# Converting a tuned kernel's weights with two VectorE steps a piece: absolute value on ScalarE, a limit on GpSimd, shift and sign on VectorE

## The chip, the cores and the metric

The kernel runs on one core of a Trainium2 chip. The metric is the device time in microseconds (us) of one execution. All runs told of here were of the fast state or, where a kernel ran once, of unknown state; a profiled run says where its time went. Engines: PE is TensorE's matmul, PEld its weight load, DVE is VectorE, ACT ScalarE, POOL GpSimd, SPq SyncE's DMA queue.

## The reference

```python
def _attn_ref(q, k, v, tau):                 # (8, 8, 576, 64) each
    scores = scale * np.matmul(q, k.transpose(0, 1, 3, 2))
    thresh = np.max(scores, axis=-1, keepdims=True) - tau
    scores = np.where(scores >= thresh, scores, -1000000000.0)
    ...                                      # softmax, times v
def _moe_ref(x, w_tok1, w_tok2, w_ch1, w_ch2):   # x is (8, 576, 512)
    h = np.maximum(x.transpose(0, 2, 1) @ w_tok1, 0.0) @ w_tok2
    u = x + h.transpose(0, 2, 1)
    return u + np.maximum(u @ w_ch1, 0.0) @ w_ch2
```

The four weight matrices are float64: a float32 array times a double-precision scalar gives float64. The kernel makes float32 out of the two 32-bit words of each weight. That conversion is all that the change touches.

## The kernel before

The weights come in 31 pieces of at most 128x512. A piece is loaded into one of four raw buffers, ScalarE shortens the low word and squares the high word, VectorE builds the bits in three steps, and GpSimd adds the low part. The function `weight(n)` issues the next n VectorE steps with what belongs to them; the loop over 144 units of attention calls it at two or three places in each unit. (The code here and below is cut: guards for pieces that are not float64 and lines that only name buffers are left out.)

```python
    def on_scalar(i, part):
            if part == 0:
                nc.scalar.activation(out=lo.bitcast(I32), in_=lo, func=AF.Copy, scale=2.0**-29)
            else:
                nc.scalar.activation(out=h2, in_=hi.bitcast(F32), func=AF.Square)

    def on_vector(i, part):
            if part == 0:        # L201: shift out three exponent bits
                nc.vector.tensor_scalar(
                    out=bits, in0=hi, scalar1=3, scalar2=0x3FFFFFFF, op0=ALU.logical_shift_left, op1=ALU.bitwise_and)
            elif part == 1:      # L205: sign and top exponent bit
                nc.vector.scalar_tensor_tensor(
                    out=bits, in0=hi, scalar=0xC0000000, in1=bits, op0=ALU.bitwise_and, op1=ALU.bitwise_or)
            else:                # L209: tiny weights become zero
                nc.vector.scalar_tensor_tensor(out=dst, in0=h2, scalar=2.0**-30, in1=dst, op0=ALU.is_ge, op1=ALU.mult)

    def on_gpsimd(i):            # L215: add the low word's part
                nc.gpsimd.tensor_tensor(out=dst.bitcast(I32), in0=dst.bitcast(I32), in1=..., op=ALU.add)

    def weight(n):
        for k in range(steps_done, min(steps_done + n, 3 * len(pieces) + 1)):
            i, part = divmod(k, 3)
            if part == 0:
                on_gpsimd(i - 1)
                if i:
                    load_piece(i - 1 + NRAW)
            else:
                on_scalar(i + 1, part - 1)
            on_vector(i, part)
            steps_done = k + 1
```

A unit, cut to the order in which things are issued (each engine runs its own instructions in this order):

```python
    for u in range(len(units) + LAG + 4):
        scores(u)                 # PE scores, DVE row maximum (mx), POOL bias
        norm(u - 1)               # DVE reciprocal (rr), POOL scaling of e
        weight(2)                 # from the second batch on; before, by a schedule
        ...
        fill(0.4)                 # PE: channel and token work of the batch before
        turn_blocks(w)            # DVE transposition T, at every third unit 16 transfers eT<-T
        weight(2)
        weigh(u)                  # ACT: e = activations of the scores, frees their PSUM
        weight(2)
```

The scores lie in PSUM, the memory that TensorE writes to. Unit 24's scores need the tiles that unit 23's activations free; so a late ScalarE holds TensorE up.

Of the kernel before, what the change touches and what calls it, by code (L numbers as in the profile page):

```python
# [9 lines left out]
F32 = mybir.dt.float32  # L10
U32 = mybir.dt.uint32
I32 = mybir.dt.int32
I64 = mybir.dt.int64
AF = mybir.ActivationFunctionType
ALU = mybir.AluOpType
# [6 lines left out]
def kernel(  # L22
# [25 lines left out]
    nc = tc.nc  # L48
# [92 lines left out]
    def like(x, dst):  # L141
# [4 lines left out]
    pieces = [  # L146
        (w1[:, 2 * i : 2 * i + 2, :], moe_w_tok1[2 * P * i : 2 * P * i + 2 * P, :].rearrange("(t p) x -> p t x", p=P))
        for i in range(NI // 2)
    ]
# [12 lines left out]



    raws = {}

    def load_piece(i):
        if i >= len(pieces):
            return
        dst, src = pieces[i]  # L170
        rows = dst.shape[0]
        n = 1
        for d in dst.shape[1:]:
            n *= d
        raw = raw_at[i % NRAW][0:rows, 0 : n * (2 if wide(i) else 1)].bitcast(src.dtype)
        nc.sync.dma_start(out=like(raw, dst), in_=src)
        if wide(i):
            words = raw.bitcast(U32).rearrange("p (n w) -> p n w", w=2)
            h2 = work.tile([P, WMAX], F32, tag="o", name=f"h2_{i}")[0:rows, 0:n]
            raws[i] = like(words[:, :, 0], dst), like(words[:, :, 1], dst), like(h2, dst)  # L180
        else:
            raws[i] = like(raw, dst)

    def wide(i):
        return i < len(pieces) and pieces[i][1].dtype == I64

    def on_scalar(i, part):
        if wide(i):
            lo, hi, h2 = raws[i]
            if part == 0:  # L190
                nc.scalar.activation(out=lo.bitcast(I32), in_=lo, func=AF.Copy, scale=2.0**-29)
            else:
                nc.scalar.activation(out=h2, in_=hi.bitcast(F32), func=AF.Square)

    def on_vector(i, part):
        if wide(i):
            dst = pieces[i][0]
            lo, hi, h2 = raws[i]
            bits = dst.bitcast(U32)
            if part == 0:  # L200
                nc.vector.tensor_scalar(  # L201
                    out=bits, in0=hi, scalar1=3, scalar2=0x3FFFFFFF, op0=ALU.logical_shift_left, op1=ALU.bitwise_and
                )
            elif part == 1:
                nc.vector.scalar_tensor_tensor(  # L205
                    out=bits, in0=hi, scalar=0xC0000000, in1=bits, op0=ALU.bitwise_and, op1=ALU.bitwise_or
                )
            else:
                nc.vector.scalar_tensor_tensor(out=dst, in0=h2, scalar=2.0**-30, in1=dst, op0=ALU.is_ge, op1=ALU.mult)  # L209

    def on_gpsimd(i):
        if i >= 0:
            dst = pieces[i][0]
            if wide(i):
                nc.gpsimd.tensor_tensor(out=dst.bitcast(I32), in0=dst.bitcast(I32), in1=raws.pop(i)[0].bitcast(I32), op=ALU.add)  # L215
            else:
                nc.gpsimd.tensor_copy(out=dst, in_=raws.pop(i))
# [3 lines left out]
    steps_done = 0  # L221

    def weight(n):

        nonlocal steps_done
        for k in range(steps_done, min(steps_done + n, 3 * len(pieces) + 1)):
            i, part = divmod(k, 3)
            if part == 0:
                on_gpsimd(i - 1)
                if i:  # L230
                    load_piece(i - 1 + NRAW)
            else:
                on_scalar(i + 1, part - 1)
            on_vector(i, part)
            steps_done = k + 1

    def weight_to(x):

        weight(max(int(x) - steps_done, 0))

    def need(i):

        weight(3 * i + 4 - steps_done)

    load_piece(0)
    load_v(0)
# [29 lines left out]
    def in_blocks(b):  # L276
        return b > 0
# [10 lines left out]
    def scores(u):  # L288
        b, p0, t = units[u]
        sc = [  # L290
            (ps_3rd if b == 0 and (2 * u + h) % 3 == 2 else ps_sc).tile([P, 2, MAIN], F32, tag="sc", name=f"sc{h}_{u}") for h in range(2)
        ]
        if t == SHARED:
            parts = [(b * NP + p0, slice(MAIN, S), slice(0, 64)), (b * NP + p0 + 1, slice(0, LAST), slice(64, P))]
        else:
            o = P * t if t < SHARED else LAST + P * (t - SHARED - 1)
            parts = [(b * NP + p0 + (t > SHARED), slice(o, o + P), slice(0, P))]
        order = [(f, part, h) for f in range(2) for part in parts for h in range(2)]
        for f, (n, cols, rows), h in order if b else sorted(order, key=lambda o: o[2]):
            r = slice(D * h, D * h + D)  # L300
            qT, kT = heads[n]
            nc.tensor.matmul(sc[h][rows, f, 0:HS], lhsT=qT[r, cols], rhs=kT[r, HS * f : HS * f + HS], start=True, stop=True)  # L302
        mx = small.tile([P, 2], F32, tag="mx", name=f"mx_{u}")
        bias = small.tile([P, 2], F32, tag="bias", name=f"bias_{u}")
        for h in range(2):
            c = slice(h, h + 1)
            nc.vector.tensor_reduce(out=mx[:, c], in_=sc[h][:, :, 0:HS], axis=AX.XY, op=ALU.max)  # L307
            nc.gpsimd.tensor_scalar(out=bias[:, c], in0=mx[:, c], scalar1=toff, scalar2=-SCALE, op0=ALU.add, op1=ALU.mult)  # L308
        st[u] = sc, bias
# [66 lines left out]
    def split_middle(n):  # L376

        lv, vl = vals[n], vlast[n % VL]
        for h in range(2):
            r = slice(D * h, D * h + D)  # L380
            nc.gpsimd.tensor_copy(out=vl[r, r], in_=lv[r, NI, :])
        vals[n] = lv, vl
# [154 lines left out]
    def values_due(u):  # L537
        while due and due[0][0] <= u:
            _, b, p0, g = due.popleft()
            values(b, p0, g)  # L540
            if p0 == NP - 2 and g == 2:
                if not in_blocks(b):
                    return True
                push(b)
        return False

    for u in range(len(units) + LAG + 4):
        on = u < len(units)
        if u == UB:
            late.close()  # L550
            ps_mm = ctx.enter_context(tc.tile_pool(name="ps_mm", bufs=2, space=bass.MemoryType.PSUM))
        if on:
            b_now, p0, t = units[u]
            n = b_now * NP + p0
        w = u - LAG
        back = 0 <= w < len(units)
        if on:
            scores(u)

        last = False  # L560
        if due and not in_blocks(due[0][1]):
            last = values_due(u)
        if 0 < u <= len(units):
            norm(u - 1)
        if b_now:
            weight(2)
        else:

            weight_to(2.25 * (u - 1.5))
        while copies:  # L570
            copies.popleft()()
        if last:
            push(0)
        if back:
            wb, wp, wt = units[w]
            if not in_blocks(wb):
                for i in range(3):
                    turn(w, i)
            if wt % GU == GU - 1:
                g = wt // GU  # L580
                if g < 2:
                    split_middle(wb * NP + wp + g)
                due.append((u + (2 if in_blocks(wb) else 1), wb, wp, g))
        if b_now:
            fill(0.4)
        if back and in_blocks(wb):
            turn_blocks(w)
        if b_now:
            weight(2)
        if on:  # L590
            weigh(u)
        elif b_now:
            fill(0.6)
        if b_now:
            weight(2)
        elif u == 0:
            on_scalar(0, 0)
            on_scalar(0, 1)
        else:
            weight_to(2.25 * (u - 1))  # L600
        if on:


            when = {3: (2, 0, 2), 4: (2, 2, 4), 5: (2, 4, 6), 6: (2, 6, 8), 8: (3, 0, 3), 0: (1, 3, 6), 1: (1, 6, 8)}
            if u == 0:
                load_qk(1, (nc.sync, nc.sync), range(0, 3))
            if t in when:
                m, lo, hi = when[t]
                if n + m < len(pairs):
                    load_qk(n + m, (nc.scalar if b_now else nc.sync,) * 2, range(lo, hi))  # L610
            if t in (3, 7) and n + 2 + t // 4 < len(pairs):
                load_v(n + 2 + t // 4)
            if t == 2:
                prep(n + 1)
            if t == 7 and n + 2 < len(pairs):
                prep(n + 2)
        if due and in_blocks(due[0][1]):
            values_due(u)
# [31 lines left out]
```

## Time and profile before

| | before |
|---|---|
| time, median (lowest to highest) | 1379.77 us (1378.82 to 1380.43), 3 runs |
| TensorE busy, of the span of 1375.1 us | 96% |
| TensorE idle from 13.75 to 206 us | 35.7 us |
| TensorE idle from 206 us to the end | 9.4 us |

The prediction shows the lines. How to read them: in the busy tenths by slice, TensorE below 9 marks the stretch in which it often waits for other engines. In an instruction row come start, duration, engine, line, operation, output and input, and in square brackets the idle time before it and what ended it.

### The profile page before, as it was taken

To read this page: it belongs to the slowest core of one execution; us is meant where nothing else is said; L and a number is where in the kernel's file an instruction comes from. 1 tells how busy PE (TensorE), PEld (TensorE's weight loads), DVE (VectorE), ACT (ScalarE), POOL (GpSimd) and SP (SyncE) were. 2 spreads that over 40 slices of the span, in tenths; PEclk is the share of its full clock that TensorE was granted. 3 is DMA by queue.
4 is the path that set the end of the run, shared out by engine and by line. 5 is a ranking of instruction groups with operands and counts; after the bars stand their busy time and mean duration, and the time that the engine had idled before them with its cause. 6 is when DMAs were issued, how large, how long until landed. Compare 5 with 4: busy or idle time off the path is not lost.

```text
span 1375.1 us, 17691 instructions
## 1 busy us (share of the span) xinstructions
PE 1322.7 (96%) x6226; PEld 817.9 (59%) x6226; DVE 588.2 (43%) x1017; ACT 581.8 (42%) x1288; POOL 356.0 (26%) x683
## 2 busy tenths in 40 slices
PE   6877799999999999999999999999999999999998
PEld 3444465646565666565665567565656576575675
DVE  6788875445444443434244444434333453201000
ACT  5666654454445444443434444353333444120110
POOL 4555653222222222222122222222121222100000
PEclk9988999999999999999999999999999999999999
DMA  5434655454544354433344435434433442400000
GB/s 121 98 96 125 183 142 124 100 123 98 122 109 114 82 121 94 113 88 95 77 100 94 113 77 123 106 83 98 103 87 75 107 103 63 115 1 16 8 11 21
DMA packets 278871, 128.20 MB, mean 93 GB/s; under 512 B 200896, under 2 KB 271552, under 8 KB 278784
## 3 DMA queue, kind: packets, MB, share of 16 engines
q1 hardware_dynamic: 150176, 111.06, 32.0%
q10 hardware_dynamic: 128608, 16.01, 7.3%
q8 instruction: 50, 0.82, 0.3%
q14 instruction: 37, 0.30, 0.1%
HBM read 43.25 MB, written 9.44 MB: 38 GB/s over the span
## 4 chain that ended last, share of the span: by engine, by line
PE 85%; DVE 7%; DMA 2%; SPq 2%; ACT 1%; issue 1%; POOL 1%; ACTq 0%; DVEq 0%; POOLq 0%
PE c L486 26%; PE c L470 26%; PE sc L302 11%; PE pv L413 9%; PE t L441 5%; PE t L448 3%; PE pv L408 3%; DVE mx L307 2%; SPq L374 2%; PE tx L432 1%; PE c L482 1%; DMA eT<-T 1%; PE tr L353 1%; DVE wc L205 1%; ACT e L317 1%
## 5 line engine op out<-in xcount | busy, mean ns | idle before, releaser
L307 DVE TENSOR_REDUCE mx<-sc 128x1 f32<-128x576 f32 x288 | 204.5, 751 | 487.9 <-PE sc L302 487.5
L470 PE MATMUL c<-xT,wc 128*128 128x256 f32 (+1 forms) x1920 | 399.4, 362 | 2.1 <-DVE xT L452 1.2
L486 PE MATMUL c<-wc,g 128*128 128x512 f32 x864 | 390.5, 597 | 0.0
L470 PEld LDWEIGHTS c<-xT,wc 128*128 128x128 f32 x1920 | 334.5, 191 | 71.5 <-issue 27.6
L308 POOL TENSOR_SCALAR bias<-mx,toff 128x1 f32<-128x1 f32 x288 | 82.8, 288 | 799.3 <-DVE mx L307 742.3
L317 ACT ACTIVATE e<-sc,bias 128x576 f32<-128x576 f32 x288 | 199.6, 739 | 162.0 <-POOL bias L308 161.4
L486 PEld LDWEIGHTS c<-wc,g 128*128 128x128 f32 x864 | 157.8, 190 | 175.7 <-issue 174.0
L471 ACT ACTIVATE g<-c 128x256 f32<-128x256 f32 (+1 forms) x240 | 86.7, 362 | 334.1 <-PE c L470 317.9
L324 ACT ACTIVATE e<-e,ntau 128x576 f32<-128x576 f32 x288 | 220.7, 771 | 0.0
L335 POOL TENSOR_SCALAR e<-e,rr 128x576 f32<-128x576 f32 x288 | 215.6, 761 | 15.8 <-DVE rr L332 4.3
L302 PE MATMUL sc<-kT,qT 64*128 64x288 f32 (+1 forms) x1280 | 196.6, 447 | 11.1 <-DVE kT L284 7.1
L365 DVE STREAM_TRANSPOSE T<-e 128x1152 f32<-128x1152 f32 x126 | 172.1, 1366 | 6.3 <-DMA eT<-T 2.6
L302 PEld LDWEIGHTS sc<-kT,qT 64*128 64x128 f32 (+1 forms) x1280 | 107.4, 184 | 98.3 <-issue 59.1
L413 PE MATMUL pv<-eT,lv 128*64 128x384 f32 (+1 forms) x1024 | 136.8, 409 | 0.0
L413 PEld LDWEIGHTS pv<-eT,lv 128*64 128x64 f32 x1024 | 76.1, 138 | 51.0 <-issue 43.6
L491 DVE COPY o<-c 128x512 f32<-128x512 f32 x36 | 24.9, 692 | 177.5 <-PE c L486 177.5
L418 ACT COPY xT<-pv 128x384 f32<-128x384 f32 (+1 forms) x56 | 21.0, 401 | 157.5 <-PE pv L413 157.5
L448 PE MATMUL t<-w,a 128*128 128x288 f32 x256 | 75.2, 421 | 7.2 <-DVE xT L452 5.3
L441 PE MATMUL t<-x_sb,w 128*128 128x512 f32 x160 | 72.1, 598 | 0.0
L448 PEld LDWEIGHTS t<-w,a 128*128 128x128 f32 x256 | 45.6, 191 | 32.2 <-issue 11.4
L452 DVE TENSOR_TENSOR xT<-xT,t 128x288 f32<-128x288 f32 x64 | 28.2, 446 | 80.5 <-PE t L448 80.0
L324 ACT ACTIVATION_READ_ACCUMULATOR e<-e,ntau 128x1 f32 x288 | 56.5, 196 | 0.0
(44 smaller groups left out, 554.7 us busy)
## 6 DMA issues: line engine op xcount, KB each, us to landing
eT<-T SPq DMA_DIRECT2D x672, 108.0 KB, 2.2
scratch<-in_moe_w_ch_dram SPq DMA_DIRECT2D x24, 512.0 KB, 3.7
lv<-in_v_dram SPq DMA_DIRECT2D x32, 288.0 KB, 3.3
out_dram<-o SPq DMA_DIRECT2D x36, 256.0 KB, 2.2
lk<-in_k_dram ACTq DMA_DIRECT2D x111, 72.0 KB, 2.6
lq<-in_q_dram ACTq DMA_DIRECT2D x106, 72.0 KB, 2.3
lq<-in_q_dram SPq DMA_DIRECT2D x22, 72.0 KB, 3.2
lk<-in_k_dram SPq DMA_DIRECT2D x17, 72.0 KB, 3.3
```

Source lines behind the costliest of these rows:

```text
L302: nc.tensor.matmul(sc[h][rows, f, 0:HS], lhsT=qT[r, cols], rhs=kT[r, HS * f : HS * f + HS], start=True, stop=True)
L307: nc.vector.tensor_reduce(out=mx[:, c], in_=sc[h][:, :, 0:HS], axis=AX.XY, op=ALU.max)
L317: nc.scalar.activation(out=eh, in_=sc[h][:, :, 0:HS], func=AF.Prelu, bias=bias[:, h : h + 1], scale=SCALE, alpha=STEEP)
L324: nc.scalar.activation(out=eh, in_=eh, func=AF.Exp, bias=ntau, accum_out=rs[:, h : h + 1])
L335: nc.gpsimd.tensor_scalar(out=eh, in0=eh, scalar1=rr[:, h : h + 1], scalar2=1.0, op0=ALU.mult, op1=ALU.mult)
L365: nc.vector.transpose(out=T[:, :, place, :].rearrange("p a (c x) -> p c a x", c=NK), in_=e.rearrange("p (c a x) -> p c a x", c=NK, a=4))
L413: nc.tensor.matmul(to[r], lhsT=lv[:, j, :], rhs=e[j], start=False, stop=(c == NI - 1), skip_group_check=True)
L441: nc.tensor.matmul(ps, lhsT=w1[:, t, P * m : P * m + P], rhs=x_sb[:, t, :], start=(t == 0), stop=(t == NT - 1))
L448: nc.tensor.matmul(ps, lhsT=s["a"][:, m, P * c : P * c + P], rhs=w2[:, m, HS * f : HS * f + HS], start=(m == 0), stop=(m == NTK - 1))
L470: nc.tensor.matmul(ps, lhsT=wc1[:, j, c, :], rhs=uT[:, c, GR * i : GR * i + n], start=(c == 0), stop=(c == NCC - 1))
L471: nc.scalar.activation(out=s["g"][:, j, 0:n], in_=ps, func=AF.Relu)
L486: nc.tensor.matmul(flat, lhsT=s["g"][:, j, P * t : P * t + P], rhs=wc2[:, j, :], start=False, stop=(j == NJ - 1), skip_group_check=True)
```

## The change

The intent is to relieve VectorE: with |high word| times 2^16 instead of the square, and a limit from below at 2.0 instead of a mask, a plain shift gives all exponent bits, and one OR adds the sign. The third VectorE step goes; the limit goes to GpSimd.

```diff
             else:
-                nc.scalar.activation(out=h2, in_=hi.bitcast(F32), func=AF.Square)
+                nc.scalar.activation(out=h2, in_=hi.bitcast(F32), func=AF.Abs, scale=2.0**16)
...
             if part == 0:
-                    out=bits, in0=hi, scalar1=3, scalar2=0x3FFFFFFF, op0=ALU.logical_shift_left, op1=ALU.bitwise_and
+                    out=bits, in0=h2.bitcast(U32), scalar1=3, scalar2=0, op0=ALU.logical_shift_left, op1=ALU.bitwise_or
-            elif part == 1:
-                    out=bits, in0=hi, scalar=0xC0000000, in1=bits, op0=ALU.bitwise_and, op1=ALU.bitwise_or
             else:
-                nc.vector.scalar_tensor_tensor(out=dst, in0=h2, scalar=2.0**-30, in1=dst, op0=ALU.is_ge, op1=ALU.mult)
+                    out=bits, in0=hi, scalar=0x80000000, in1=bits, op0=ALU.bitwise_and, op1=ALU.bitwise_or
+
+    def on_gpsimd_first(i):
+            nc.gpsimd.tensor_scalar(out=h2, in0=h2, scalar1=2.0, scalar2=1.0, op0=ALU.max, op1=ALU.mult)
...
-            i, part = divmod(k, 3)
+            i, part = divmod(k, 2)
             if part == 0:
                 on_gpsimd(i - 1)
                 if i:
                     load_piece(i - 1 + NRAW)
-            else:
-                on_scalar(i + 1, part - 1)
+            on_scalar(i + 1, 1 - part)
             on_vector(i, part)
+            if part:
+                on_gpsimd_first(i + 1)
...
         if b_now:
-            weight(2)          # at the second and the third place of a unit
+            weight(1)
```

(The calls in the first batch change from 2.25 to 1.5 steps a unit. Pieces a unit stay the same everywhere.)

More of the change, by code (lines that the diff above doesn't have):

```diff
@@ L201, in on_vector @@
                 nc.vector.tensor_scalar(
-                    out=bits, in0=hi, scalar1=3, scalar2=0x3FFFFFFF, op0=ALU.logical_shift_left, op1=ALU.bitwise_and
-                )
-            elif part == 1:
-                nc.vector.scalar_tensor_tensor(
-                    out=bits, in0=hi, scalar=0xC0000000, in1=bits, op0=ALU.bitwise_and, op1=ALU.bitwise_or
-                )
-            else:
-                nc.vector.scalar_tensor_tensor(out=dst, in0=h2, scalar=2.0**-30, in1=dst, op0=ALU.is_ge, op1=ALU.mult)
+                    out=bits, in0=h2.bitcast(U32), scalar1=3, scalar2=0, op0=ALU.logical_shift_left, op1=ALU.bitwise_or
+                )
+            else:
+                nc.vector.scalar_tensor_tensor(
+                    out=bits, in0=hi, scalar=0x80000000, in1=bits, op0=ALU.bitwise_and, op1=ALU.bitwise_or
+                )
+    def on_gpsimd_first(i):
+        if wide(i):
+            h2 = raws[i][2]
+            nc.gpsimd.tensor_scalar(out=h2, in0=h2, scalar1=2.0, scalar2=1.0, op0=ALU.max, op1=ALU.mult)
     def on_gpsimd(i):
@@ L225, in weight @@
         nonlocal steps_done
-        for k in range(steps_done, min(steps_done + n, 3 * len(pieces) + 1)):
-            i, part = divmod(k, 3)
+        for k in range(steps_done, min(steps_done + n, 2 * len(pieces) + 1)):
+            i, part = divmod(k, 2)
             if part == 0:
@@ L241, in need @@
     def need(i):
-        weight(3 * i + 4 - steps_done)
+        weight(2 * i + 3 - steps_done)
     load_piece(0)
@@ L567 @@
         else:
-            weight_to(2.25 * (u - 1.5))
+            weight_to(1.5 * (u - 1.5))
         while copies:
@@ L594 @@
         if b_now:
-            weight(2)
+            weight(1)
         elif u == 0:
@@ L598 @@
             on_scalar(0, 1)
+            on_gpsimd_first(0)
         else:
-            weight_to(2.25 * (u - 1))
+            weight_to(1.5 * (u - 1))
         if on:
```

## The prediction

> **What bounds the kernel now.** I read the page's busy shares first, then its slices, then a table of busy time by stretch, then the groups and instructions of the stretch that the change touches.
>
> ```profile
> PE 1322.7 (96%) x6226; PEld 817.9 (59%) x6226; DVE 588.2 (43%) x1017; ACT 581.8 (42%) x1288; POOL 356.0 (26%) x683
> ...
> PE   6877799999999999999999999999999999999998
> ...
> DVE  6788875445444443434244444434333453201000
> ```
>
> TensorE is busy 96% of the span, so over most of it nothing that VectorE saves can count. Only the first six slices (34 us each, to 206 us) show TensorE at 6 to 8 tenths with VectorE at 7 to 8. There the weights are converted: 31 pieces, the last three-step piece at 198 us. After that TensorE is the bound, so a microsecond of TensorE idleness won or lost before 206 us should arrive at the end nearly whole.
>
> ```profile
> 13.75:106.18 92.43, 74.25 (x434) 44.42 (x432) 74.68 (x159) 62.53 (x131) 52.69 (x86) 0.91 0.38 86
> 106.18:206.00 99.82, 82.29 (x380) 50.76 (x379) 83.89 (x129) 62.99 (x131) 59.13 (x68) 0.91 0.59 154
> ```
>
> This is busy time of PE, PEld, DVE, ACT, POOL in two stretches, then the clock. From 13.75 to 106 us (the first pair of batches) TensorE is idle 18 us of 92, from 106 to 206 us 17.5 us of 100. So 35 us, 2.6% of the run, is all that a perfect conversion could win.
>
> In the second stretch VectorE and GpSimd stand in each other's way. One unit of attention there, VectorE in order of time, then GpSimd:
>
> ```profile
> 138.49 0.65 DVE L209 SCALAR_TENSOR_TENSOR wc<-h,wc 128x512 f32<-128x512 f32 x1
> 139.06 1.51 DVE L201 TENSOR_SCALAR wc<-scratch 128x512 uint32<-128x512 uint32 x1
> 140.60 1.66 DVE L205 SCALAR_TENSOR_TENSOR wc<-scratch,wc 128x512 uint32<-128x512 uint32 x1
> 142.37 0.69 DVE L209 SCALAR_TENSOR_TENSOR wc<-h,wc 128x512 f32<-128x512 f32 x1
> ```
> ```profile
> 138.49 3.22 POOL L215 TENSOR_TENSOR wc<-wc,scratch 128x512 int32<-128x512 int32 x2
> ```
>
> The shift takes 0.41 us alone and 1.51 here; the OR 0.70 alone and 1.66 here: each waits until one GpSimd addition is over.
>
> The third view is ScalarE and the SP DMA queue around the first block transposition:
>
> ```profile
> 148.63 12.19 SPq L374 DMA_DIRECT2D eT<-T  x16
> 160.93 19.33 SPq L176 DMA_DIRECT2D scratch<-in_moe_w_ch_dram  x6
> 180.48 10.38 SPq L374 DMA_DIRECT2D eT<-T  x16
> 190.97 0.52 SPq L176 DMA_DIRECT2D scratch<-in_moe_w_ch_dram  x1
> ```
> ```profile
> 154.55 0.74 ACT L317 ACTIVATE e<-sc,bias 128x576 f32<-128x576 f32 x1 [0.82 <-POOL bias L308]
> ...
> 165.20 0.69 ACT L191 ACTIVATE scratch<-scratch 128x512 int32<-128x512 uint32 x1 [2.82 <-DMA scratch<-in_moe_w_ch_dram]
> ```
>
> Sixteen transfers of T hold the queue 10 to 12 us; the weight load behind them (piece 24, issued 160.93) lands only at 165.2, and piece 30 (issued 190.97) at 194.6. ScalarE, in order, waits for each, but in the kernel before this comes **behind** its activations of unit 23 (154.55), so they are not held.
>
> **What the Trainium skill says.** "SBUF — State Buffer", section "Who interferes with whom": VectorE and GpSimd share a port pair as an exclusive lock; a VectorE instruction in a 2-port mode, or with two SBUF inputs against a GpSimd reader, blocks or is blocked for the whole instruction. The 1.51 and 1.66 us above agree. "VectorE: DVE Perf Modes", section "Mode 2×_2P": a one-source fp32 tensor_scalar in SBUF makes two results a cycle; the shift's 0.41 against the OR's 0.70 us fits. So both remaining VectorE steps can still be blocked. "ScalarE: Activation LUTs", section "Table sets: the hidden batching unit": abs lies in every table set; the trace has one table load, and the built instruction stream of the changed kernel has one too, so Abs for Square should cost nothing.
>
> **The change part by part.**
>
> Removed: the masking multiply L209, 31 times, 24 pieces at a mean of 0.83 us (20.0 us) and 7 smaller (4.0 us): 24 us of VectorE. Kept: shift and OR, at the old durations. Changed on ScalarE: Abs for Square, 0.66 us each, no difference. Added: a GpSimd tensor_scalar per piece. From L335, 128x576 in 0.73 us alone, I take 0.66 us for 512 columns and 0.4 for 288: about 19 us of GpSimd.
>
> First stretch (12 pieces, 1.5 steps a unit in place of 2.25). The chain that ended last, read from 10 to 106 us, holds 3.2 us of L201, 3.8 of L205 and 2.1 of L209, 9 us in all. One step in three goes: about 3 us won. Piece 0's limit now stands before unit 1's bias on GpSimd, about 0.7 us lost. Net -2.5 us.
>
> Second stretch (19 pieces, two a unit). Before, a unit from 114.74 to 123.29 us has VectorE full. After it: reduction 1.42, reciprocal 0.4, shift and OR 1.1, copies or transposition 1.4. Then the second shift waits for GpSimd: norm 1.97, addition 1.3, limit 0.7 put that at about 4.3 us after the reciprocals begin, where the second addition (1.3) takes the lock. Shift, OR and a collision with the next limit bring the next reduction at 8.4 to 8.9 us, against 8.55. So the saved VectorE step is **lost to the lock and to the wait for the limit**: 0, give or take 3 us over the stretch.
>
> Order on ScalarE. The instruction order of the built changed kernel shows the Abs of the second piece of a unit *ahead* of that unit's attention activations. Before, the first touch of that piece (the low words' conversion) stood behind them. All loads keep their place on the SP queue. So at unit 23 the activations that could start at 154.55 must wait for piece 24 (165.2) plus 0.66 us: 11 us late. They free the PSUM tiles for unit 24's scores, done before at 161.89; these come at about 167.1, 5.2 us late, of which TensorE's old 0.77 us wait is regained: **+4.5 us**. At unit 26 the same with piece 30: activations from 184.86 go to about 195.3, the next scores from 186.38 to 196.7, 10.3 us late, less 1.6 and 0.9 us of old TensorE idleness: **+7.8 us**. Units without these transfers lose at most 0.6 us each, mostly hidden.
>
> Sum: -2.5 + 0 + 4.5 + 7.8 = +9.8 us; I shade it to +8.7, because the few microseconds of chain that VectorE saves in the second stretch may not all be lost. 1379.8 + 8.7 = **1388.5 us**.
>
> **The rivals.**
>
> (a) The intended one: VectorE bounds the first 200 us and its step is saved. For it: VectorE at 81 and 84% busy in the two stretches, and the chain of the second gives L205 8.5%, L209 5.1% and L201 4.2%. If all L209 time on the chain (2.1 us, then 5.1% of 100 us) were won and nothing lost: about 1372 us. Against it: the lock, and ScalarE's order.
>
> (b) GpSimd becomes the bound. Its maximum may be slower than the multiplication from which I took 0.66 us. At twice that, two limits a unit add 1.3 us to a chain that already paces the unit: +6 to +12 us over nine units, 1395 to 1400 us.
>
> (c) The late load is hidden anyway: TensorE has other channel work in units 23 and 26. Against it: that work's results are evacuated by the same blocked ScalarE through two PSUM buffers, so TensorE runs dry after two. If hidden all the same, 1377 to 1380 us.
>
> **Range and chances.** The stalls carry most of the doubt (5 to 16 us), the gain the rest (0 to 8 us): 1378 to 1399 us should hold it 8 times in 10. Two per cent is 27.6 us: slower by that needs (b) and both stalls together, faster needs nearly all of the 35 us of idleness. Chances: faster 0.01, within 2% 0.96, slower 0.03.
>
> **What would show it right or wrong.** Right: VectorE's total falls by 15 to 24 us and GpSimd's rises by about 19, while the span does not fall; ScalarE shows two waits of 7 us or more on the weight loads in front of the Abs line, near 155 to 165 and 189 to 199 us, with TensorE idle, released by ScalarE, behind them; the shift shows durations near 1.5 us. TensorE's idleness between 137 and 206 us grows from 10.8 us to above 20. Wrong: no such ScalarE waits (then the DMA order differs from what I read), limits longer than 0.9 us, a second table load, or a first stretch shorter by over 6 us.

## The result, and the profile after

The changed kernel took 1401.78 us in the median (1400.73 to 1405.09, 6 runs), the kernel before 1380.10 us beside it (6 runs). Ratios here are the mean time of one kernel's fast runs over that of the other's fast runs of the same rounds, so not quite the ratio of the medians; this one is 1.0158 (95% interval 1.0141 to 1.0175). The result is right. The change costs 21.7 us by the medians, and the measured time lies above the predicted range.

Busy shares and slices of the changed kernel's page:

```profile
PE 1328.6 (95%) x6226; PEld 820.6 (59%) x6226; DVE 565.5 (40%) x986; ACT 581.4 (42%) x1288; POOL 406.4 (29%) x714
...
PE   5877679999999999999999999999999999999998
...
POOL 4778883323232222222221222222222222100000
```

VectorE lost 22.7 us of work, as intended. GpSimd gained 50.4, where the prediction had 19. TensorE now has six thin slices of 35 us, where it had five (its sixth slice before reads 9), and in the last three of them GpSimd is busier than TensorE itself. The same two stretches as before (PE, PEld, DVE, ACT, POOL busy):

```profile
13.75:106.18 92.43, 68.14 (x382) 40.65 (x381) 64.45 (x137) 60.67 (x128) 66.08 (x94) 0.92 0.38 86
106.18:206.00 99.82, 75.01 (x337) 45.76 (x333) 62.42 (x105) 53.24 (x107) 84.52 (x81) 0.89 0.48 131
```

TensorE does 6.1 and 7.3 us less in the same times, GpSimd goes from 59 to 84.5 us in the second. After 240 us the two kernels do the same: TensorE is idle 8.9 us from there to the end, 9.4 us from 206 us on before.

Not all of the loss is waiting. Between the two profiled runs the span grows by 25.0 us, TensorE's idle time by 19.1 (from 52.4 to 71.5) and its busy time by 5.9, for the same 6226 matmuls. TensorE's mean granted clock over the first 240 us was 0.90, against 0.93 before; a score matmul of 288 columns took 403 ns in the median where the full clock was granted and 684 where half was. No experiment here sets the clock, so what lowers it stays open.

One unit of the second stretch, first on VectorE, then on GpSimd:

```profile
146.93 1.37 DVE L370 STREAM_TRANSPOSE T<-e 128x1152 f32<-128x1152 f32 x1
151.43 1.51 DVE L202 TENSOR_SCALAR wc<-h 128x512 uint32<-128x512 uint32 x1 [3.13 <-POOL h L213]
152.98 0.98 DVE L206 SCALAR_TENSOR_TENSOR wc<-scratch,wc 128x512 uint32<-128x512 uint32 x1
```
```profile
148.23 1.27 POOL L219 TENSOR_TENSOR wc<-wc,scratch 128x512 int32<-128x512 int32 x1
149.48 1.91 POOL L213 TENSOR_SCALAR h<-h 128x512 f32<-128x512 f32 x1
151.37 1.29 POOL L219 TENSOR_TENSOR wc<-wc,scratch 128x512 int32<-128x512 int32 x1
152.64 2.08 POOL L213 TENSOR_SCALAR h<-h 128x512 f32<-128x512 f32 x1
```

VectorE sits idle 3.13 us for the limit, is then blocked behind the addition (1.51 us for a shift of 0.41), and GpSimd runs without a gap: the limit takes 1.91 us where the prediction took 0.66. But the limit does not block VectorE for all of its time: the OR at 152.98 began 0.34 us into a limit of 2.08 us and took 0.98 us, and it took the same 0.98 beside the multiplication of 0.79 us of experiment e4. So, as far as the traces show, what hurts is that the limit's result comes late and that other GpSimd work stands behind it.

On ScalarE the two stalls that the prediction named are there:

```profile
174.59 0.67 ACT L194 ACTIVATE h<-scratch 128x512 f32<-128x512 f32 x1 [9.77 <-DMA scratch<-in_moe_w_ch_dram]
175.16 1.35 ACT L322 ACTIVATE e<-sc,bias 128x576 f32<-128x576 f32 x2
...
210.66 0.66 ACT L194 ACTIVATE h<-scratch 128x512 f32<-128x512 f32 x1 [9.98 <-DMA scratch<-in_moe_w_ch_dram]
211.22 1.36 ACT L322 ACTIVATE e<-sc,bias 128x576 f32<-128x576 f32 x2
```

TensorE's scores wait behind them. Who waited for whom (us in total, times, longest), before up to 206 us and changed up to 225 us:

```profile
PE sc L302 <- ACT e L317: 3.9, 4, 1.9
```
```profile
PE sc L307 <- ACT e L322: 15.2, 6, 9.3
```

Where the loss builds up is best seen from the start of each unit's row maximum on VectorE, counted from that of unit 0 in the same run. Microseconds more (or less) than the kernel before, which starts unit 18 at 96.8, unit 23 at 144.0, unit 24 at 153.8, unit 27 at 182.0 us; the last column is the difference of the medians at the end. "Early order" means that the first ScalarE step on a unit's second piece is issued ahead of the unit's activations, as in the changed kernel; "late order" that it is issued behind them, as in the kernel before:

| kernel | unit 18 | unit 23 | unit 24 | unit 27 | end |
|---|---|---|---|---|---|
| changed | +7.4 | +12.9 | +17.1 | +22.7 | +21.7 |
| changed, no limit (e1) | -5.3 | -4.8 | +3.2 | +10.2 | +9.0 |
| changed, late order (e2) | +9.7 | +19.9 | +25.0 | +26.0 | +25.1 |
| no limit and late order (e3) | -5.7 | -9.4 | -10.0 | -7.9 | -9.7 |
| multiplication for the maximum (e4) | -0.5 | +0.1 | +4.9 | +12.7 | +11.2 |
| before, early order (e6) | +2.1 | +3.3 | +8.4 | +16.2 | +14.3 |
| before, one GpSimd maximum more (e7) | +8.5 | +25.1 | +28.8 | +38.9 | +30.9 |

The stalls on the weight loads lie between units 23 and 24 and from unit 26 on. (The end is from all timed runs, the units from one profiled run of each kernel. That of the kernel before took 1376.94 us, 3 to 5 us under its medians in the timed rounds; at the end of the profiled spans the rows stand at +25.0, +14.8, +26.6, -4.2, +15.4, +18.4 and +36.0. So a unit's number can be some 2 to 6 us too high, and steps along a row are surer than its level.)

### The profile page after: what moved, and what is told of

Read it like the earlier page. It is cut to its first block, busy times and chain, and to the rows that moved or that the text cites. A ratio compares the mean times of both kernels' runs of the same rounds, so it can differ in the third digit from the quotient of the medians.

```text
span 1400.1 us, 17676 instructions
## 1 busy us (share of the span) xinstructions
PE 1328.6 (95%) x6226; PEld 820.6 (59%) x6226; DVE 565.5 (40%) x986; ACT 581.4 (42%) x1288; POOL 406.4 (29%) x714
## 4 chain that ended last, share of the span: by engine, by line
PE 85%; DVE 5%; POOL 4%; ACT 2%; DMA 2%; SPq 1%; issue 1%; DVEq 0%; POOLq 0%; ACTq 0%
PE c L475 26%; PE c L491 25%; PE sc L307 11%; PE pv L418 9%; PE t L446 5%; PE t L453 3%; PE pv L413 3%; DVE mx L312 3%; POOL h L213 2%; POOL e L340 1%; PE tx L437 1%; PE c L487 1%; SPq L379 1%; DMA eT<-T 1%; POOL wc L219 1%
## 5 line engine op out<-in xcount | busy, mean ns | idle before, releaser
L340 POOL TENSOR_SCALAR e<-e,rr 128x576 f32<-128x576 f32 x288 | 216.4, 763 | 16.5 <-DVE rr L337 4.9
L453 PE MATMUL t<-w,a 128*128 128x288 f32 x256 | 75.7, 423 | 10.2 <-DVE xT L457 8.1
L453 PEld LDWEIGHTS t<-w,a 128*128 128x128 f32 x256 | 45.9, 192 | 35.4 <-issue 12.2
L213 POOL TENSOR_SCALAR h<-h 128x512 f32<-128x512 f32 (+2 forms) x31 | 57.5, 1856 | 6.9 <-ACT h L194 6.7
```

The source lines that it names most:

```text
L340: nc.gpsimd.tensor_scalar(out=eh, in0=eh, scalar1=rr[:, h : h + 1], scalar2=1.0, op0=ALU.mult, op1=ALU.mult)
L453: nc.tensor.matmul(ps, lhsT=s["a"][:, m, P * c : P * c + P], rhs=w2[:, m, HS * f : HS * f + HS], start=(m == 0), stop=(m == NTK - 1))
```

## The experiments

**Theory T** at the start: two causes that add up, the length of GpSimd's limit and ScalarE's order. **Rival G**: the limit alone, the ScalarE waits being its consequence. **Rival S**: ScalarE's order alone.

### e1: no limit

```diff
-            nc.gpsimd.tensor_scalar(out=h2, in0=h2, scalar1=2.0, scalar2=1.0, op0=ALU.max, op1=ALU.mult)
+            pass
```

> The changed kernel without GpSimd's limit (right on this data, where no weight is small enough to be limited; wrong in general). Theory T, two causes that add (limit 1.92 us an instruction, some 12 us; and the order on ScalarE, some 13 us): 1388 us, with both ScalarE waits of about 10 us on the weight loads still there. Rival G, GpSimd's limit alone is the cause and the ScalarE waits follow from it: 1374 to 1379 us. Rival S, ScalarE's order alone is the cause: about 1400 us.

Measured: 1390.87 us, ratio to before 1.0062 (1.0042 to 1.0083). Its ScalarE keeps both stalls:

```profile
164.11 0.66 ACT L194 ACTIVATE h<-scratch 128x512 f32<-128x512 f32 x1 [10.25 <-DMA scratch<-in_moe_w_ch_dram]
...
199.40 0.66 ACT L194 ACTIVATE h<-scratch 128x512 f32<-128x512 f32 x1 [8.77 <-DMA scratch<-in_moe_w_ch_dram]
```

Rival G falls: with no limit the kernel still loses 9 us, all of it from unit 23 on. Up to there it is 5 us ahead of the kernel before.

### e2: late order on ScalarE, limit kept

```diff
-            on_scalar(i + 1, 1 - part)
+            if part:
+                on_scalar(i + 1, 1)
+                on_scalar(i + 1, 0)
             on_vector(i, part)
```

> The changed kernel with both ScalarE steps of a piece issued at its second VectorE step, so that the second piece of a unit is touched behind that unit's attention activations as in the kernel before; limit kept. Theory T: 1387 to 1391 us, ScalarE waits in front of the unit's activations gone, VectorE's waits for the limit (about 30 us in all) still there. Rival G: 1400 us. Rival S: 1376 to 1381 us.

Measured: 1406.95 us, ratio 1.0175 (1.0152 to 1.0197). Neither T nor S: the late order does not help at all as long as the limit is there. From its list of who waited for whom (us in total, times, longest):

```profile
DVE wc L202 <- POOL h L213: 35.4, 14, 3.4
...
POOL h L213 <- ACT h L194: 24.4, 10, 5.6
```

The ScalarE stalls in front of the activations went, but now GpSimd's limit waits for the later Abs, 24.4 us in all, and what stands behind it in GpSimd's order waits too. One such place, GpSimd's next rows:

```profile
189.09 1.92 POOL L213 TENSOR_SCALAR h<-h 128x512 f32<-128x512 f32 x1 [5.62 <-ACT h L194]
190.99 0.27 POOL L315 TENSOR_SCALAR bias<-mx,toff 128x1 f32<-128x1 f32 x1
```

The bias of the next unit's activations stands behind the limit. So the two causes do not add; T has to be amended: **the limit's length and the place of its input on ScalarE act on one in-order GpSimd queue**. (This is read from the trace; e8 tests it.)

### e3: no limit and late order

Both edits together.

> Both undone: no limit, late order. Theory T: the saved VectorE step is then won, 1372 to 1377 us, under the kernel before. Rival G: the same as without the limit alone. Rival S: the same as late order alone. If a third cause exists, it stays over 1380 us.

Measured: 1372.15 us, ratio 0.9927 (0.9904 to 0.9951). As expected by T: the VectorE step that the change saves is worth something, once nothing is paid for it. The four kernels together: without the limit the early order costs 18.7 us (1390.87 against 1372.15); with the limit it costs nothing (1401.78, in another run, against 1406.95).

### e4: a multiplication in the maximum's place

```diff
-            nc.gpsimd.tensor_scalar(out=h2, in0=h2, scalar1=2.0, scalar2=1.0, op0=ALU.max, op1=ALU.mult)
+            nc.gpsimd.tensor_scalar(out=h2, in0=h2, scalar1=1.0, scalar2=1.0, op0=ALU.mult, op1=ALU.mult)
```

> The changed kernel with the GpSimd instruction's max replaced by a multiplication by 1.0, shape and place the same (right on this data). If max is what makes the instruction slow: 0.66 us for 512 columns and about 1389 us in all, which is what the prediction said. If the immediate scalars or the place make it slow: 1.9 us and 1400 us.

Measured: 1393.02 us, ratio 1.0077 (1.0056 to 1.0097). The group in the stretch from 106 to 206 us, of e4 and then of the changed kernel (busy us, mean ns):

```profile
L213 POOL TENSOR_SCALAR h<-h 128x512 f32<-128x512 f32 x18 | 11.8, 653 | 12.5 <-ACT h L194 12.5
```
```profile
L213 POOL TENSOR_SCALAR h<-h 128x512 f32<-128x512 f32 x19 | 37.6, 1978 | 0.5 <-ACT h L194 0.5
```

Same shape, same place: 0.65 us, as the prediction assumed, against 1.98. With that duration the whole kernel comes out 11.2 us slower than before, 4 us over what was expected of this run; the prediction's sum was +9.8, shaded to +8.7.

### e5: a scale that needs no limit

```diff
-                nc.scalar.activation(out=h2, in_=hi.bitcast(F32), func=AF.Abs, scale=2.0**16)
+                nc.scalar.activation(out=h2, in_=hi.bitcast(F32), func=AF.Abs, scale=2.0**-112)
```

on top of e3. The shift drops the sign and the two top exponent bits and moves the third into the sign's place, so the exponent's change counts only modulo 64, and +16 and -112, which differ by 128, are the same there; but with -112 a weight too small for float32 falls to zero or near it by itself.

> A candidate that needs no limit: as both undone, but Abs with a scale of 2^-112 in place of 2^16, so that exponents too small for float32 fall to zero or to tiny values by themselves (weights under 2^-119 may be lost, an error no larger than that; everything else has the same bits after the shift). Theory T: the same instructions as with both undone, so 1372 us (1370 to 1375), faster than before by 0.5 to 0.9%, and right. If ScalarE treats such a scale in another way, the result is wrong or the durations differ from 0.66 us.

Measured: right, 1373.47 us, ratio 0.9945 (0.9923 to 0.9967, 6 runs against 11). It beats both kernels: 7.0 us, or 0.5%, under the kernel before by the medians. How such a gain splits is not settled: in e5's profiled run TensorE is idle 45.6 us, against 52.4 in the kernel before, at the same busy time; in e3's, with the same instructions, it is idle 53.5 us, but busy 5.3 us less, at a mean granted clock of 0.994 against 0.988. No weight here is small enough to show how ScalarE treats results in the denormal range; the bound of 2^-119 is worked out from the arithmetic, not run.

### e6: the kernel before with the early order

```diff
-            else:
-                on_scalar(i + 1, part - 1)
+            if part < 2:
+                on_scalar(i + 1, part)
             on_vector(i, part)
```

> The kernel before with only ScalarE's order changed: each of its two steps of a piece is issued one VectorE step earlier, so that the second piece of a unit is touched ahead of that unit's attention activations. Theory T: the order alone costs 12 to 19 us, 1392 to 1399 us, with two ScalarE waits of about 10 us. Rival G (the order matters only with the new arithmetic): 1379 to 1382 us.

Measured: 1394.79 us, ratio 1.0105 (1.0079 to 1.0131). The order alone, with the old arithmetic, costs 14.3 us, and the two stalls appear:

```profile
167.92 0.65 ACT L191 ACTIVATE scratch<-scratch 128x512 int32<-128x512 uint32 x1 [10.92 <-DMA scratch<-in_moe_w_ch_dram]
...
203.99 0.65 ACT L191 ACTIVATE scratch<-scratch 128x512 int32<-128x512 uint32 x1 [9.82 <-DMA scratch<-in_moe_w_ch_dram]
```

### e7: the kernel before with one more GpSimd maximum

```diff
                 on_gpsimd(i - 1)
+                on_gpsimd_first(i)      # nc.gpsimd.tensor_scalar(h2, h2, 0.0, 1.0, ALU.max, ALU.mult): changes nothing
```

> The kernel before with one more GpSimd instruction a piece, a maximum with 0 of the squares, which changes nothing in the result: GpSimd's cost alone, without any other part of the change. Theory T: 1.9 us an instruction, GpSimd 50 us busier, VectorE waiting for it, 1388 to 1398 us. Rival S: hidden, 1379 to 1383 us.

Measured: 1411.39 us, ratio 1.0225 (1.0198 to 1.0251), more than expected. The maximum alone costs 30.9 us here, with the kernel before's late order and all three VectorE steps. Up to 240 us its VectorE waited 46.6 us for it. Why it costs more than in the changed kernel was not tested. Rival S falls with this: the maximum is not hidden.

### e8: late order with the multiplication

e2 with e4's edit.

> Late order with the multiplication by 1.0 in the limit's place (0.62 us for 512 columns in the run with the early order). Tells whether the late order failed with the limit because of the limit's length, or because GpSimd's queue then waits for ScalarE: if length, 1373 to 1380 us; if the wait for ScalarE, over 1385 us.

Measured: 1381.73 us, ratio 1.0001 (0.9971 to 1.0032), just over the range for length, well under the other. Against no instruction at all (e3, ratio 0.9927) a GpSimd instruction of 0.65 us in that place costs about 0.7%, some 10 us; the maximum there (e2, 1.0175) costs 2.5%. Most of it is length, but GpSimd still waited 33.3 us for ScalarE's Abs in this run.

### e9, e10, e11: which form is slow

The GpSimd instruction alone was changed; one look each, durations from the profile (median of the 128x512 ones between 106 and 206 us).

```diff
-            ... scalar1=2.0, scalar2=1.0, op0=ALU.max, op1=ALU.mult
+e9          ... scalar1=2.0, scalar2=None, op0=ALU.max
+e10         ... scalar1=1.0, scalar2=2.0, op0=ALU.mult, op1=ALU.max
+e11         ... scalar1=1.0, scalar2=0.0, op0=ALU.mult, op1=ALU.add
```

> The changed kernel with the maximum as the only step of the GpSimd instruction (no multiplication by 1.0 after it). If a maximum itself is slow on GpSimd: about 1.9 us for 512 columns, 1401 us. If only the pair of max and mult is: 0.6 us, and about 1393 us.

> The two steps exchanged: multiplication by 1.0, then the maximum. If a maximum is slow wherever it stands: about 1.9 us for 512 columns; if only as first step: 0.6 us.

> Multiplication by 1.0, then addition of 0.0. If only max is slow: 0.6 us for 512 columns as with two multiplications; if two multiplications are a special fast case: 1.9 us.

| instruction | 128x512, us | kernel, us (one run) |
|---|---|---|
| max, mult (the change) | 1.92 | 1401.78, median of 6 |
| e10: mult, max | 1.92 | 1402.14 |
| e9: max alone | 1.49 | 1399.73 |
| e11: mult, add | 0.62 | 1393.26 |
| e4: mult, mult | 0.62 | 1393.02, median of 4 |

The maximum is the slow part, alone or in either place; alone it took less than the 1.9 us expected of it. Times from single runs are not more than a check.

### e12: the load ahead of the transfers

On top of e1 (no limit, early order):

```diff
+        if b_now:
+            weight(1)
         if back and in_blocks(wb):
             turn_blocks(w)
-        if b_now:
-            weight(1)
```

> The changed kernel without the limit (1391 us in its own run), ScalarE's early order kept, but the unit's third conversion step issued just ahead of the block transposition, so that the weight load stands before the sixteen eT transfers on the SP queue and not behind them. If the ScalarE stalls come from the load's place on that queue: both 9 to 10 us waits gone or under 4 us, 1371 to 1379 us. If the early order costs by itself (the extra step ahead of the activations), 1386 to 1391 us.

Measured: 1382.14 us, ratio 1.0008 (0.9986 to 1.0030), between the two expectations. A little under half of the early order's 18.7 us went with the load's place on the SP queue (1390.87 to 1382.14 us in different runs, 8.7 us; 7.5 us by the ratios). Of the two long stalls one is left, of 6.50 us, and ScalarE's waits on weight loads before 230 us come to 15.9 us in seven, against 28.8 in seven without this edit. What the remaining 10 us over e3 are made of is open: the shorter waits in front of the activations, or the transfers of eT, which now stand behind a load that itself waits for GpSimd. No run separates these.

## Why the prediction was wrong, point by point

**The bound and where it lies: right.** The whole difference arose before 240 us, while TensorE was not full. (A slip without effect on the sum: the prediction speaks of six thin slices up to 206 us, but its PE line shows five, and 9 in the sixth.) That all of the loss would be idleness did not hold: 5.9 of 25.0 us were longer busy time at a lower clock.

**The GpSimd limit: the step that failed.** The prediction's words were "From L335, 128x576 in 0.73 us alone, I take 0.66 us for 512 columns and 0.4 for 288: about 19 us of GpSimd." That was a multiplication's duration, carried over to a maximum. Measured: 1.92 us and 57.5 us in all. e4 put the assumed 0.65 us in its place and the whole kernel fell to 1393.02 us, inside the predicted range: of the 13.0 us by which the change cost more than the predicted 8.7, the limit's length accounts for 10.5 (21.7 less 11.2). The rival (b) named this very risk, but at twice the multiplication; it was three times.

**First stretch, predicted -2.5 us.** It was mis-sized in both terms. Without the limit (e1) unit 18 comes 5.3 us earlier (5.7 in e3), so the saved step is worth more than the 3 us that I read from the chain. But even a limit of 0.65 us gives most of it back (e4: -0.5), not the 0.7 us that I counted for the first unit alone; probably because it stands in GpSimd's order before later work in every unit, which no run isolates. At 1.92 us unit 18 comes 7.4 us late.

**Second stretch up to unit 23, predicted 0.** The path was right, through norm, addition, limit and the lock, and with a 0.65 us limit the sum was right too (e4: from -0.5 to +0.1). With 1.92 us VectorE waited for the limit up to 3.2 us at a time, 28.2 us in all for the channel weights, and 5.5 us more were lost. The "collision with the next limit" was small: an OR beside a limit took 0.98 us.

**Abs for Square on ScalarE: right.** Both took 0.66 us for 128x512, and each trace has one table load.

**ScalarE's order, predicted +4.5 and +7.8 us.** Right in mechanism and near in size: the changed kernel loses 4.2 us between units 23 and 24, and 5.9 us between 26 and 27 with 3 more at unit 28. e6 shows it alone, at 14.3 us against the 12.3 predicted. What I had not seen is that it does not add to the limit's cost (e1, e2, e3): with the order mended the limit waits for ScalarE and the bias waits behind it.

**The rivals.** (a) The intended gain: it exists, 9.7 us in e3 (ratio 0.9927), near the 1372 us that I wrote for it, but not in this form. (b) was what happened, on top of the stalls. (c) Hidden anyway: refuted by e6. The signs: VectorE lost 22.7 us, the two ScalarE waits were 9.8 and 10.0 us (at 165 to 175 and 201 to 211 us) with TensorE waiting behind them, and 7 of the 20 shifts after 100 us took near 1.5 us; but TensorE's idleness from 137 to 206 us grew only from 10.9 to 16.5 us, the second wait lying partly later, and one sign of being wrong came, limits longer than 0.9 us. Range and chances: the kernel stayed within 2% (1.6% slower), but I gave (b) too little weight; the largest new instruction had no row of its own kind in the trace of before, and the range should have been wider for that.

## What to carry to other kernels

Before moving work to another engine, find a row of that very operation on that engine in a trace, or measure one: a maximum cost three times a multiplication of the same shape, and that turned a saved VectorE step into a new bound. When steps are regrouped, read each engine's new instruction order for what now stands ahead of urgent work: a first touch of a late transfer placed ahead of the activations cost 14 us without any change of arithmetic. And test two suspected causes in all four combinations, for mending one alone may show nothing.

## What the Trainium skill lacked or had wrong

- "GPSIMD Engine Reference", section "3.1 Elementwise — side-by-side cycle accounting": it gives an add of two tensors, a best case of 768 ns for 512 elements and, for its smallest loop bodies, a port-bound 1.03 cycles an element, but no cost by operation for one input and a constant; section "4.1 Engine selection" has add, mul and max in one row and calls one input "roughly line-rate". Here 128x512 fp32 took 0.62 us for mult-mult and mult-add, under the 768 ns, but 1.49 us for a maximum alone and 1.92 us for a maximum with a multiplication: the maximum does not belong in that row.
- "SBUF — State Buffer", section "Who interferes with whom": agreed with for the addition: a VectorE shift of 0.41 us took 1.51 us when a GpSimd addition of 1.29 us had begun just before it. Not for the limit: by its section "Summary: rules for kernel authors" a VectorE instruction with two SBUF inputs that comes second "fully blocks" until the first finishes, but the OR, which has two, took 0.98 us when it began 0.34 us into a limit of 2.08 us, one of five such places in the changed kernel's trace.
- No page gives how long transfers of this shape hold the issuing queue on this chip: sixteen eT transfers held SP's queue 10.4 to 12.2 us in the kernel before, and the weight load issued behind the first sixteen was usable 16.6 us after their start (148.63 to 165.20).
